# Reordering the last chunks of a recurrence's first stretch, with shared move queues and the weights' low parts on another engine

## The chip, the core and the metric

The kernel runs on one core of a Trainium2 chip. Its engines are TensorE (PE), VectorE (DVE), ScalarE (ACT), GpSimd (POOL) and SyncE (SP); each works through its own queue of instructions in order. SP issues most DMA transfers, ACT a few; an issue takes its place in the queue of the engine that makes it. The metric is the device time of one execution in microseconds (us), as the median of several runs.

## What is computed

```python
# gated recurrence, state 48x48 for each of 4 batches x 8 heads, 768 steps
state = alpha[:, :, t, :, None] * state + einsum('bhd,bhe->bhde', k[:, :, t], v[:, :, t])
y[:, :, t] = einsum('bhd,bhde->bhe', q[:, :, t], state)
x = y as (3072 tokens, 384)
h = x @ w_in                                  # 384 -> 2048
x = (h * sigmoid(h)) @ w_out                  # 2048 -> 384
out = (sigmoid(x @ w_gate) * (x @ w_val)) @ w_out2   # 384 -> 1536 -> 384
```

Everything is float32. The weights arrive as 64-bit numbers and are turned into float32 on the chip.

## The kernel before

**Chunks.** The recurrence is cut into 24 chunks of 128 tokens. For a chunk `c`, `prep` multiplies keys and queries by decay products (two scans and a product on DVE, the queries' product on POOL for the first nine chunks). `full_scores` makes the transposed keys and the scores on PE, `full_scores_done` masks the scores on DVE (line 478) and copies the keys on ACT (line 481), and `full_results` makes the chunk's output `y` and its state update `u` on PE (lines 496 to 517). `full_state` (lines 530 and 533) takes `u` over into the state on DVE and so frees its PSUM place. `y_out` copies `y` to SBUF on ACT (line 552); after each second chunk it also issues six small DMAs, the moves (line 560), which bring 16 rows each to other partitions. `x_out` then splits the two chunks' output into a high part (ACT, line 578, which waits for the moves) and a low part (DVE, line 579).

**First stretch.** Chunks 0 to 8 (`LEAD` is 9) run with whole chunks, 0 to 5 in a loop, and 6, 7 and 8 in code of their own. Queue order is exactly the order of the code (`manual_schedule`). The block of chunk 7 (`c = LEAD - 2`) begins with `x_out(c - 2)`, which is for chunks 4 and 5; that of chunk 8 begins with the first matmul group of the MLP for token block 0 (`early`), and holds `x_out(c - 1)` for chunks 6 and 7.

**Mixed stretch.** Then PE runs the first MLP for token blocks 0 and 1 in an alternating list of 26 items (b, f), f being one of 16 slices of the hidden width: nine matmuls of `mm_in` give `h` (three for each of three slices of the input, high and low parts), ACT makes the Silu `g` (line 741) and its high part `gh` (749), DVE the low part `gl` (750), and nine matmuls of `mm_out` add to the output two items later. Block 1 is made of chunks 4 to 7, so the second group needs what both `x_out` calls give. The pool of `h` has two places, shared with `u` and the transposed keys.

**Weights.** Meanwhile `way1` converts one pair of weight tiles after another: `in` slice j and `out` slice j-1. ACT scales (line 629), DVE rebuilds the number (lines 635 and 637; then, after ACT's line 656, lines 668, 670 and 671), ACT rounds to the high part (line 660, two instructions), POOL subtracts to get the low part (line 678, two instructions). In the first stretch this goes by `bit()`, a quarter of a pair, and in the mixed stretch by `half()`, half a pair at each item, with extra halves after the items in `MORE`. `way2` does the same for the second MLP's weights, much later.

Of the kernel before, what the change touches and what calls it, by code (L numbers as in the profile page):

```python
# [7 lines left out]
F32 = mybir.dt.float32  # L8
# [6 lines left out]
ALU = mybir.AluOpType  # L15
# [23 lines left out]
LEAD = 9  # L39
# [2 lines left out]


BITS = 4
MORE = (3, 10, 16)

FIRST = {"T": (1, 11, 0), "scores": (1, 12, 0)}
VISIT = {9: (1, 12, 1), 10: (1, 13, 0), 11: (1, 14, 0)}
# [139 lines left out]
def gated_attention_then_mlps(ctx: ExitStack, tc: tile.TileContext, qka, a0, v, w_in, w_out, w_gate, w_val, w_out2, out):  # L188
    nc = tc.nc
# [15 lines left out]
    def X(i, dtype=F32):  # L205

        return xp.tile([P, NK, N], dtype, tag=f"x{i}", name=f"x{i}", bufs=1)
# [21 lines left out]
    def load_decays(c):  # L229

        if c < NC:
            qk[c] = places[c % 4]
            nc.sync.dma_start(out=qk[c][:, K_OFF:], in_=qka[c][:, K_OFF:])

    def load_queries(c):
        nc.sync.dma_start(out=qk[c][:, :K_OFF], in_=qka[c][:, :K_OFF])
# [9 lines left out]
    def load_values(c):  # L246
        vt[c] = ap.tile([P, H, D], F32, tag="v", name="v", bufs=4)
        nc.sync.dma_start(out=vt[c], in_=v[c].rearrange("t (h e) -> t h e", e=D))
# [20 lines left out]
    def two_banks(g):  # L269
        return ps_g[g].tile([P, 2, N], F32, tag="s", name=f"s{g}")  # L270
# [14 lines left out]
    def check(c, i):  # L285

        x = (Gt, At)[i].pop(c, None)
        if x is None:
            return
        nc.scalar.activation(x, x, AF.Square, accum_out=chk[:DP, c, i : i + 1])  # L290
# [34 lines left out]
    def last_of(c):  # L325
        return c % CB == CB - 1
# [126 lines left out]
    def full_scores(c, g, p0=0, p1=NP):  # L453

        t = qk[c]
        if p0 == 0:
            S[c] = two_banks(g)
            if not last_of(c):
                T[c] = ps_h.tile([P, N], F32, tag="h", name="t")
        for p in range(p0, p1):  # L460
            if not last_of(c):
                nc.tensor.transpose(T[c][:, p * DP : (p + 1) * DP], t[:, NP * C + p * C : NP * C + (p + 1) * C], ident)
        for p in range(p0, p1):
            for j in range(2):
                r = 64 * j
                nc.tensor.matmul(
                    S[c][:, j, p * C : (p + 1) * C],
                    t[r : r + D, NP * C + p * C : NP * C + (p + 1) * C],
                    t[r : r + D, p * C : (p + 1) * C],
                    start=True,  # L470
                    stop=True,
                )

    def full_scores_done(c):
        for_all = causal.rearrange("s (i t) -> s i t", i=1).to_broadcast([P, NP, C])
        M[c] = M_lead[c % 2]
        for j in range(2):
            nc.vector.tensor_tensor(M[c][j], S[c][:, j].rearrange("s (i t) -> s i t", i=NP), for_all, op=ALU.mult)
        if not last_of(c):
            KT[c] = ap.tile([P, NP, DP], F32, tag="kt", name="kt", bufs=2)  # L480
            nc.scalar.activation(KT[c], T.pop(c)[:, : NP * DP].rearrange("t (p d) -> t p d", p=NP), AF.Copy)
        check(c, 0)
        check(c, 1)

# [50 lines left out]
    def block_of(c):  # L535
        for b, (t0, n) in enumerate(BLOCKS):
            if t0 <= c * C < t0 + n:
                return b, c * C - t0
        raise ValueError(c)
# [3 lines left out]
    def y_out(c):  # L543

        m, o = divmod(c, 2)
        if o == 0:
            xf[m] = ap.tile([P, NP, 2, C], F32, tag="x", name="x", bufs=2)
        x = xf[m]
        if c < LEAD:
            y = Y.pop(c)[:DP].rearrange("r (p t) -> r p t", p=NP)  # L550
            for lo, hi in ((NK, NP), (0, NK)):
                nc.scalar.activation(x[:DP, lo:hi, o], y[:, lo:hi], AF.Copy)
        else:
            y_halves(c, x, o)
        if o:
            for j in range(2):
                r = 64 * j
                for i in range(NK):
                    by = nc.scalar if j and c in (LEAD - 2, LEAD + 2) else nc.sync
                    by.dma_start(out=x[r + D : r + 64, i], in_=x[r + 16 * i : r + 16 * (i + 1), NK])  # L560

    def y_halves(c, x, o):

        yu = YU.pop(c)[0][:, :, :UA].rearrange("r h (p t) -> r h p t", p=NP)
        nc.scalar.activation(x[:DP, :, o, :HC], yu[:DP, 0], AF.Copy)
        for j in range(2):
            r, at = 64 * j, 64 * (1 - j)
            nc.scalar.activation(x[r : r + D, :, o, HC:], yu[at : at + D, 1], AF.Copy)

    def x_out(c):  # L570
        if c % 2 == 0:
            return
        b, o = block_of(c - 1)
        if o == 0:
            xh[b], xl[b] = (X(i, F32R) for i in x_at[b])
        x = xf.pop(c // 2)[:, :NK].rearrange("r k c t -> r k (c t)")
        h, l = (y[b][:, :, o : o + 2 * C] for y in (xh, xl))
        nc.scalar.activation(h, x, AF.Copy, accum_out=chk[:, c, 2:3])
        nc.vector.tensor_tensor(l, x, h.bitcast(F32), op=ALU.subtract)


# [8 lines left out]
    SW = NK * P  # L590

    class Way:
# [80 lines left out]
        def b_rest(self, j):  # L673
            if self.has(j):
                _, _, b, _ = self.views(j)
                for i, key in enumerate(self.pairs[j]):
                    h, l = (wslot[key][:, x].rearrange("p k c -> p (k c)") for x in range(2))
                    nc.gpsimd.tensor_tensor(l, b[:, i * SW : (i + 1) * SW].bitcast(F32), h.bitcast(F32), op=ALU.subtract)  # L678
                self.raw.pop(j), self.tmp.pop(j)

        def bit(self):
# [37 lines left out]
    def mm3(ps, w, k, x_h, x_l, first, last):  # L719

        wh, wl = w[:, 0, k, :], w[:, 1, k, :]
        nc.tensor.matmul(ps, wh, x_l, start=first, stop=False)  # L722
        nc.tensor.matmul(ps, wh, x_h, start=False, stop=False)  # L723
        nc.tensor.matmul(ps, wl, x_h, start=False, stop=last)  # L724
# [7 lines left out]
    def mm_in(pool, tag, name, b, f):  # L732
        h = pool.tile([P, N], F32, tag=tag, name=tag)
        for k in range(NK):
            mm3(h, wslot[name, f], k, xh[b][:, k, :], xl[b][:, k, :], k == 0, k == NK - 1)
        return h
# [86 lines left out]
    with tc.manual_schedule():  # L823
        way1 = Way(
            [[key for key in (("in", j), ("out", j - 1)) if 0 <= key[1] < NF1] for j in range(NF1 + 1)],
            lambda j: X(2 * j % 4, U32).rearrange("p k t -> p (k t)"),
            lambda j: X(2 * j % 4 + 1, U32).rearrange("p k t -> p (k t)"),
            lambda n: wp.tile([P, 2, NK, P], F32R, tag="w", name="w"),
        )
# [41 lines left out]
        def states():  # L871
            while late and (late[0] + 1 == LEAD or last_of(late[0]) or late[0] + 1 in AE):
                c = late.pop(0)
                if not last_of(c):
                    full_state(c)
# [6 lines left out]
        for s in range(4):  # L882
            prep(1, s)
        full_scores_done(0)

        def computed(c):
            full_results(c, c % 2)
            late.append(c)

        def taken(c):  # L890
            load_queries(c + 4)
            load_values(c + 4)
            y_out(c)

        for c in range(LEAD - 3):
            full_scores(c + 1, (c + 1) % 2)
            load_decays(c + 5)
            if c > 2:
                states()
            prep(c + 2, 0)  # L900
            states()
            for s in range(1, 4):
                prep(c + 2, s)
            full_scores_done(c + 1)
            if c > 1:
                x_out(c - 2)
            computed(c)
            if c == 2:
                way1.a_scalar(0)
            taken(c)  # L910
            if c == 0:
                way1.load(1)
            if c > 2:
                way1.bit()


        c = LEAD - 3
# [4 lines left out]
        prep(c + 2, 0)  # L922
        prep(c + 2, 1)
        computed(c)
        states()
        prep(c + 2, 2)
        prep(c + 2, 3)
# [2 lines left out]


        c = LEAD - 2
        x_out(c - 2)
        computed(c)
        way1.bit()
        full_scores(c + 1, (c + 1) % 2)
        load_decays(c + 5)
        taken(c)
        states()
        way1.bit()  # L940
        full_scores_done(c + 1)


        c = LEAD - 1
        early = {(0, 0): mm_in(ps_h, "h", "in", 0, 0)}
        computed(c)
        x_out(c - 1)
        way1.bit()
        states()
        taken(c)  # L950
        for _ in range(3):
            way1.bit()
        way1.n_half = 2 * (way1.n_bits // BITS)

        def steps(items):

# [81 lines left out]
        for i, (b, f) in enumerate(items):  # L1038
# [7 lines left out]
            h = early.pop((b, f), None) or mm_in(ps_h, "h", "in", b, f)  # L1046
# [9 lines left out]
            others(i, 1)  # L1056
            if i in MORE:
                way1.half(True)
# [81 lines left out]
```

## Time and profile before

| what | value |
|---|---|
| median of 3 runs | 960.63 us (959.96 to 961.23) |
| the profiled execution | 961.75 us, of which 959.9 us are the span of its instructions |
| PE busy | 930.9 us (97%) |
| DVE busy | 457.2 us (48%) |
| ACT busy | 391.0 us (41%) |
| POOL busy | 114.7 us (12%) |
| mean granted clock of PE | 0.989 of 2.4 GHz |

Times of rows count from the first instruction. In a timeline row stand start, duration, engine, line, operation, output and inputs, and in brackets how long the engine had been idle before and what released it. SPq and ACTq are DMA issues in those engines' queues.

### The profile page before, as it was taken

What the parts mean: (1) busy time and instruction counts of PE and PEld (TensorE: products, weight loads), DVE (VectorE), ACT (ScalarE), POOL (GpSimd) and SP (SyncE); (2) the same over time, 40 slices, a digit from 0 to 9 for tenths busy, and PEclk for the clock granted to TensorE, in tenths of its full rate; (3) what the DMA queues carried; (4) which work ended last, traced back from release to release, by engine and by line L of the source; (5) the groups of instructions that cost most, each with busy time, mean ns of one, the idle gap of its engine ahead of it and who ended that gap; (6) DMA issues with size and microseconds to landing.
All of it is one profiled execution on the core that took longest, in us unless ns stands there. A gap on an engine that the chain in (4) does not pass through costs nothing.

```text
span 959.9 us, 14882 instructions
## 1 busy us (share of the span) xinstructions
PE 930.9 (97%) x6164; PEld 763.8 (80%) x6164; DVE 457.2 (48%) x682; ACT 391.0 (41%) x725; POOL 114.7 (12%) x109
## 2 busy tenths in 40 slices
PE   7869999999999999999999999999999999999997
PEld 5647888787888888878888888888888888888885
DVE  8858999545534444514675444433222232232221
ACT  3447666454444444435566444433122222222211
POOL 3224444100000000000322111110000000000000
PEclk8989999999999999999999999999999999999999
DMA  9763232041221120004222212001000000000001
GB/s 230 206 181 132 99 104 78 23 119 38 60 62 39 42 59 3 5 1 136 99 93 73 66 66 67 1 1 66 1 0 34 1 1 12 22 1 1 33 1 36
DMA packets 35355, 54.95 MB, mean 57 GB/s; under 512 B 3856, under 2 KB 24368, under 8 KB 35280
## 3 DMA queue, kind: packets, MB, share of 16 engines
q1 hardware_dynamic: 34704, 53.47, 18.6%
q8 instruction: 50, 0.82, 0.4%
q10 hardware_dynamic: 576, 0.46, 0.2%
q14 instruction: 25, 0.20, 0.1%
HBM read 48.02 MB, written 4.72 MB: 55 GB/s over the span
## 4 chain that ended last, share of the span: by engine, by line
PE 88%; DVE 4%; DMA 3%; issue 2%; POOL 1%; ACT 1%; SPq 0%; DVEq 0%; ACTq 0%; POOLq 0%
PE h L722 13%; PE h L724 13%; PE h L723 13%; PE s L722 5%; PE s L724 5%; PE s L723 5%; PE o L724 3%; PE o L722 3%; PE o L723 3%; PE v L722 3%; PE v L723 3%; PE v L724 3%; PE y L722 3%; PE y L724 3%; PE y L723 3%
## 5 line engine op out<-in xcount | busy, mean ns | idle before, releaser
L722 PE MATMUL h<-x,w 128*128 128x512 f32 x582 | 229.5, 394 | 8.5 <-DVE state L533 3.7
L724 PE MATMUL h<-x,w 128*128 128x512 f32 x582 | 228.0, 392 | 1.0 <-POOL w L678 1.0
L723 PE MATMUL h<-x,w 128*128 128x512 f32 x582 | 228.2, 392 | 0.0
L750 DVE TENSOR_TENSOR gl<-g,gh 128x512 fp32r<-128x512 f32 x168 | 123.7, 736 | 191.6 <-ACT gh L749 191.6
L749 ACT ACTIVATE gh<-g 128x512 fp32r<-128x512 f32 x168 | 106.2, 632 | 160.4 <-DVE g L744 157.4
L722 PEld LDWEIGHTS h<-x,w 128*128 128x128 f32 x582 | 110.0, 189 | 33.2 <-DVE state L533 3.9
L724 PEld LDWEIGHTS h<-x,w 128*128 128x128 f32 x582 | 110.1, 189 | 25.0 <-POOL w L678 1.5
L723 PEld LDWEIGHTS h<-x,w 128*128 128x128 f32 x582 | 110.2, 189 | 22.9
L744 DVE TENSOR_TENSOR g<-v,g 128x512 f32<-128x512 f32 x46 | 31.8, 692 | 178.7 <-PE v L724 178.7
L741 ACT ACTIVATE g<-h 128x512 f32<-128x512 f32 x96 | 56.9, 593 | 128.9 <-PE h L724 128.9
L743 ACT ACTIVATE g<-h 128x512 f32<-128x512 f32 x72 | 43.1, 598 | 136.3 <-PE h L724 136.3
L722 PE MATMUL s<-gl,w 128*128 128x512 f32 x240 | 95.4, 398 | 0.1
L724 PE MATMUL s<-gh,w 128*128 128x512 f32 x240 | 93.6, 390 | 0.0
L723 PE MATMUL s<-gh,w 128*128 128x512 f32 x240 | 93.6, 390 | 0.0
L678 POOL TENSOR_TENSOR w<-tmp,w 128x384 fp32r<-128x384 f32 x36 | 40.9, 1158 | 207.4 <-ACT w L660 207.4
L678 POOL TENSOR_TENSOR w<-x,w 128x384 fp32r<-128x384 f32 x32 | 50.0, 1579 | 70.5 <-ACT w L660 70.5
L722 PE MATMUL o<-gl,w 128*128 128x512 f32 x144 | 56.2, 390 | 0.0
L724 PE MATMUL o<-gh,w 128*128 128x512 f32 x144 | 56.2, 390 | 0.0
L723 PE MATMUL o<-gh,w 128*128 128x512 f32 x144 | 56.1, 390 | 0.0
L744 DVE TENSOR_TENSOR g<-h,g 128x512 f32<-128x512 f32 x26 | 18.0, 691 | 79.8 <-PE h L724 79.8
L722 PE MATMUL v<-x,w 128*128 128x512 f32 x138 | 54.0, 391 | 0.0
L723 PE MATMUL v<-x,w 128*128 128x512 f32 x138 | 53.9, 390 | 0.0
(141 smaller groups left out, 1288.6 us busy)
## 6 DMA issues: line engine op xcount, KB each, us to landing
x<-in_moe_w_in SPq DMA_DIRECT2D x16, 384.0 KB, 3.4
x<-in_moe_w_out SPq DMA_DIRECT2D x16, 384.0 KB, 3.8
x<-in_qka SPq DMA_DIRECT2D x12, 448.0 KB, 4.4
qk<-in_qka SPq DMA_DIRECT2D x11, 448.0 KB, 6.1
v<-in_v SPq DMA_DIRECT2D x24, 192.0 KB, 4.9
raw<-in_moe_w_gate SPq DMA_DIRECT2D x12, 384.0 KB, 3.8
raw<-in_moe_w_val SPq DMA_DIRECT2D x12, 384.0 KB, 3.8
raw<-in_moe_w_out SPq DMA_DIRECT2D x12, 384.0 KB, 3.8
```

The lines of the kernel that those rows point to most:

```text
L678: nc.gpsimd.tensor_tensor(l, b[:, i * SW : (i + 1) * SW].bitcast(F32), h.bitcast(F32), op=ALU.subtract)
L722: nc.tensor.matmul(ps, wh, x_l, start=first, stop=False)
L723: nc.tensor.matmul(ps, wh, x_h, start=False, stop=False)
L724: nc.tensor.matmul(ps, wl, x_h, start=False, stop=last)
L741: nc.scalar.activation(g, h, AF.Silu)
L743: nc.scalar.activation(g, h, AF.Sigmoid)
L744: nc.vector.tensor_tensor(g, val, g, op=ALU.mult)
L749: nc.scalar.activation(gh, g, AF.Copy)
L750: nc.vector.tensor_tensor(gl, g, gh.bitcast(F32), op=ALU.subtract)
```

## The change

It has three parts. Its own line numbers stand 2 to 8 above those of before: 533 becomes 535, 552 554, 560 562, 578 580, 579 587, 629 637, 635 643, 637 645, 656 664, 660 668, 668 676, 670 678, 671 679, 678 686, 741 749, 749 757, 750 758.

1. Order in the last chunks. For chunk 7, `x_out(5)` moves behind `computed(7)` and a conversion quarter, and its DVE half is put off to chunk 8 (`x_rest`); `y_out(7)` goes ahead of the loads of chunks 11 and 12. For chunk 8, a conversion quarter and `states()` go ahead of `x_out(7)`; two quarters are left out and become half a pair in the mixed stretch (`n_half` 3 in place of 4, `MORE` with four entries). The squares that check overflow (`checks`) go behind `y_out(8)` for chunk 8.
2. Of the six moves after chunks 1, 3 and 5, three are now issued by ACT, as was so after chunk 7.
3. The weights' low parts are subtracted by DVE for all pairs but the first of each way.

```diff
-MORE = (3, 10, 16)
+MORE = (3, 10, 15, 21)
...
-                    by = nc.scalar if j and c in (LEAD - 2, LEAD + 2) else nc.sync
+                    by = nc.scalar if j and (c < LEAD or c == LEAD + 2) else nc.sync
...
-    def x_out(c):
+    def x_out(c, rest=None):
...
+        if rest is not None:
+            rest.append((l, x, h))
+        else:
+            x_rest(l, x, h)
+
+    def x_rest(l, x, h):
         nc.vector.tensor_tensor(l, x, h.bitcast(F32), op=ALU.subtract)
...
-                    nc.gpsimd.tensor_tensor(l, b[:, i * SW : (i + 1) * SW].bitcast(F32), h.bitcast(F32), op=ALU.subtract)
+                    (nc.vector if j else nc.gpsimd).tensor_tensor(l, b[:, i * SW : (i + 1) * SW].bitcast(F32), h.bitcast(F32), op=ALU.subtract)
...
         c = LEAD - 2
-        x_out(c - 2)
         computed(c)
         way1.bit()
+        rest = []
+        x_out(c - 2, rest)
         full_scores(c + 1, (c + 1) % 2)
+        y_out(c)
         load_decays(c + 5)
-        taken(c)
+        load_queries(c + 4)
+        load_values(c + 4)
         states()
         way1.bit()
         full_scores_done(c + 1)
...
         c = LEAD - 1
+        x_rest(*rest[0])
         early = {(0, 0): mm_in(ps_h, "h", "in", 0, 0)}
+        way1.bit()
         computed(c)
+        states()
         x_out(c - 1)
         way1.bit()
-        states()
         taken(c)
-        for _ in range(3):
-            way1.bit()
-        way1.n_half = 2 * (way1.n_bits // BITS)
+        way1.a_scalar(2)
+        checks(c)
+        way1.n_half = 3
```

PE's own order does not change. DVE's order from chunk 8's second scan on, before (`state` by 533 frees chunk 7's `u`, 530 chunk 8's; the two 579 are `x_out` for chunks 5 and 7):

```order
L316 SCALAR_TENSOR_TENSOR A<-qk_92,d_89 112x512
L579 TENSOR_TENSOR x_635<-x,x_634 128x3x256
L635 TENSOR_SCALAR x_666<-x_666 128x768
L533 TENSOR_TENSOR state_88<-u,aend 112x192
L637 SCALAR_TENSOR_TENSOR x_666<-x_666 128x768
L478 TENSOR_TENSOR m_98<-s_669,causal 128x512
L478 TENSOR_TENSOR m_99<-s_669,causal 128x512
L579 TENSOR_TENSOR x_635<-x,x_634 128x3x256
L668 TENSOR_SCALAR x_666<-x_666 128x768
L670 TENSOR_TENSOR x_666<-x_666 128x768
L671 TENSOR_TENSOR x_666<-x_666 128x768
L530 COPY state_88<-u 112x192
```

and the same place of the change:

```order
L316 SCALAR_TENSOR_TENSOR A<-qk_92,d_89 112x512
L643 TENSOR_SCALAR x_662<-x_662 128x768
L535 TENSOR_TENSOR state_88<-u,aend 112x192
L645 SCALAR_TENSOR_TENSOR x_662<-x_662 128x768
L478 TENSOR_TENSOR m_98<-s_668,causal 128x512
L478 TENSOR_TENSOR m_99<-s_668,causal 128x512
L587 TENSOR_TENSOR x_666<-x,x_665 128x3x256
L676 TENSOR_SCALAR x_662<-x_662 128x768
L678 TENSOR_TENSOR x_662<-x_662 128x768
L679 TENSOR_TENSOR x_662<-x_662 128x768
L532 COPY state_88<-u 112x192
L587 TENSOR_TENSOR x_666<-x,x_665 128x3x256
```

The subtraction for chunk 5 moved behind the state of chunk 7 and the masks of chunk 8, and that for chunk 7 behind the conversion and the state of chunk 8.

ACT's order from `x_out` for chunk 5 to the first Silu, before:

```order
L578 ACTIVATE x_634,chk<-x 128x3x256
L629 ACTIVATE x_666<-x_242 128x768
L552 ACTIVATE x<-y_638 112x128
L552 ACTIVATE x<-y_638 112x3x128
L560 DMA x<-x 16x256 x3
L656 ACTIVATE x_666<-x_242 128x768
...
L578 ACTIVATE x_634,chk<-x 128x3x256
L660 ACTIVATE w<-x_666 128x384 x2
...
L656 ACTIVATE x_763<-x_511 128x768
L741 ACTIVATE g<-h 128x512
```

and in the change:

```order
L637 ACTIVATE x_662<-x_242 128x768
L580 ACTIVATE x_665,chk<-x 128x3x256
L554 ACTIVATE x<-y_634 112x128
L554 ACTIVATE x<-y_634 112x3x128
L562 DMA x<-x 16x256 x3
L664 ACTIVATE x_662<-x_242 128x768
L481 ACTIVATE kt<-t 128x448
L668 ACTIVATE w<-x_662 128x384 x2
L580 ACTIVATE x_665,chk<-x 128x3x256
...
L290 ACTIVATE A,chk<-A 112x512
L749 ACTIVATE g<-h 128x512
```

The scaling by 629 now stands ahead of the wait for chunk 5's moves, the rounding to high parts ahead of the wait for chunk 7's, and no line 656 stands right ahead of the first Silu; two checks stand there.

On DVE, one round of the mixed stretch before (one pair, two items):

```order
L668 TENSOR_SCALAR x_780<-x_780 128x768
L670 TENSOR_TENSOR x_780<-x_780 128x768
L671 TENSOR_TENSOR x_780<-x_780 128x768
L750 TENSOR_TENSOR gl<-g,gh 128x512
L635 TENSOR_SCALAR x_829<-x_829 128x768
L637 SCALAR_TENSOR_TENSOR x_829<-x_829 128x768
L750 TENSOR_TENSOR gl<-g,gh 128x512
```

and in the change:

```order
L676 TENSOR_SCALAR x_761<-x_761 128x768
L678 TENSOR_TENSOR x_761<-x_761 128x768
L679 TENSOR_TENSOR x_761<-x_761 128x768
L758 TENSOR_TENSOR gl<-g,gh 128x512
L686 TENSOR_TENSOR w<-x_761,w 128x384 x2
L643 TENSOR_SCALAR x_796<-x_796 128x768
L645 SCALAR_TENSOR_TENSOR x_796<-x_796 128x768
L758 TENSOR_TENSOR gl<-g,gh 128x512
```

The two subtractions stand in DVE's queue behind each second `gl`; POOL's queue has none of them.

## Rows read from the trace of the kernel before

**Rows 1.** Timeline of PE, four idle times around the first `h` groups:

```profile
53.43 1.16 PE L466 MATMUL s<-qk 48*128 48x128 f32 x16
58.34 0.79 PE L722 MATMUL h<-x,w 128*128 128x512 f32 x1 [3.75 <-DVE state L533]
...
64.17 1.08 PE L517 MATMUL y<-qk,state 48*64 48x128 f32 x16
68.38 0.80 PE L722 MATMUL h<-x,w 128*128 128x512 f32 x1 [3.12 <-DVE state L530]
...
73.60 0.50 PE L722 MATMUL h<-x,w 128*128 128x512 f32 x1 [1.30 <-ACT g L741]
```

**Rows 2.** Busy time by stretch: PE, PEld, DVE, ACT, POOL, then PEclk, DMA share, GB/s:

```profile
34.10:51.80 17.70, 14.06 (x194) 11.35 (x192) 17.53 (x28) 8.91 (x26) 3.44 (x4) 0.90 0.88 235
68.40:71.80 3.40, 3.40 (x8) 2.73 (x9) 1.36 (x2) 1.97 (x5) 1.97 (x2) 0.50 0.06 19
73.60:168.00 94.40, 94.33 (x414) 77.56 (x414) 88.79 (x109) 64.70 (x113) 44.17 (x29) 1.00 0.32 105
400.00:760.00 360.00, 359.74 (x1741) 295.99 (x1740) 155.15 (x225) 144.78 (x239) 40.89 (x36) 1.00 0.14 47
```

**Rows 3.** Timeline of ACT between chunk 7 and the first Silu:

```profile
55.62 0.84 ACT L578 ACTIVATE x<-x 128x768 fp32r<-128x768 f32 x1 [5.58 <-DMA x<-x]
56.47 0.89 ACT L629 ACTIVATE x<-x 128x768 f32<-128x768 f32 x1
57.26 0.64 ACT L552 ACTIVATE x<-y 112x128 f32<-112x128 f32 x2
57.55 1.90 ACTq L560 DMA_DIRECT2D x<-x  x3
59.49 0.91 ACT L656 ACTIVATE x<-x 128x768 bf16<-128x768 uint16 x1 [1.59 <-DVE x L637]
...
60.73 0.62 ACT L290 ACTIVATE G<-G 112x512 f32<-112x512 f32 x1
...
64.07 0.84 ACT L578 ACTIVATE x<-x 128x768 fp32r<-128x768 f32 x1 [2.02 <-DMA x<-x]
68.09 0.94 ACT L660 ACTIVATE w<-x 128x384 fp32r<-128x384 f32 x2 [3.08 <-DVE x L671]
72.96 0.58 ACT L741 ACTIVATE g<-h 128x512 f32<-128x512 f32 x1
```

**Rows 4.** Timeline of DVE in the same stretch:

```profile
57.94 0.35 DVE L533 TENSOR_TENSOR state<-u,aend 112x192 f32<-112x192 f32 x1
65.04 0.96 DVE L579 TENSOR_TENSOR x<-x,x 128x768 fp32r<-128x768 f32 x1 [4.69 <-ACT x L578]
```

**Rows 5.** Timeline of SP, the six moves after chunk 5:

```profile
46.04 6.92 SPq L560 DMA_DIRECT2D x<-x  x6
```

**Rows 6.** Groups of DVE from 73.6 to 170: count, busy us, mean ns, idle before:

```profile
L750 DVE TENSOR_TENSOR gl<-g,gh 128x512 fp32r<-128x512 f32 x24 | 23.1, 962 | 1.4 <-ACT gh L749 1.4
L637 DVE SCALAR_TENSOR_TENSOR x<-x 128x768 uint32<-128x768 uint32 x13 | 19.4, 1493 | 0.4
L671 DVE TENSOR_TENSOR x<-x 128x768 f32<-128x768 f32 x14 | 13.4, 958 | 0.5
...
L670 DVE TENSOR_TENSOR x<-x 128x768 bf16<-128x768 bf16 x14 | 7.8, 558 | 1.8 <-ACT x L656 0.4
```

**Rows 7.** Timelines of POOL and of DVE, with and without POOL at work:

```profile
75.52 2.76 POOL L678 TENSOR_TENSOR w<-x,w 128x384 fp32r<-128x384 f32 x2 [4.86 <-ACT w L660]
75.75 1.65 DVE L637 SCALAR_TENSOR_TENSOR x<-x 128x768 uint32<-128x768 uint32 x1
97.69 0.96 DVE L637 SCALAR_TENSOR_TENSOR x<-x 128x768 uint32<-128x768 uint32 x1
98.57 0.69 DVE L750 TENSOR_TENSOR gl<-g,gh 128x512 fp32r<-128x512 f32 x1
```

**Rows 8.** From PE's waits over the span (total, times, longest):

```profile
PE h L724 <- POOL w L678: 1.0, 1, 1.0
```

More of the change, by code (lines that the diff above doesn't have):

```diff
@@ L481, in full_scores_done, with checks @@
             nc.scalar.activation(KT[c], T.pop(c)[:, : NP * DP].rearrange("t (p d) -> t p d", p=NP), AF.Copy)
+    def checks(c):
         check(c, 0)
@@ L884, in gated_attention_then_mlps @@
         full_scores_done(0)
+        checks(0)
         def computed(c):
@@ L904, in gated_attention_then_mlps @@
             full_scores_done(c + 1)
+            checks(c + 1)
             if c > 1:
@@ L924, in gated_attention_then_mlps @@
         computed(c)
+        checks(c + 1)
         states()
```

## Prediction

> **What bounds the kernel now.** I read PE's waits first, then PE's timeline at the places they name, then ACT's and DVE's timelines there. From 73.6 to 168 us PE is busy 94.33 of 94.40 us at full clock [rows 2], and over the whole span the list of its waits names little behind that but one wait of 1.0 us for a low part of the weights, late in the mixed stretch [rows 8]. So time can be won only ahead of 73.6, and at that one wait. Ahead of 73.6 PE stands idle three times: 3.75 us ahead of the first `h` group, 3.12 ahead of the second, 1.30 ahead of the third [rows 1]. The first two groups also run slowly: the second takes 73.60 - 1.30 - 68.38 = 3.92 us, the granted clock from 68.4 to 71.8 being 0.50, 1.2 GHz [rows 2]; at full clock nine matmuls take 9 x 94.40 / 414 = 2.05 us.
>
> Why PE waits is seen on ACT and DVE. The scores of chunk 8 are done at 54.59 [rows 1], but `u` of chunk 7 is freed only at 57.94 + 0.35 [rows 4]: DVE's subtraction for chunk 5 stands ahead of it and waits for ACT's line 578, which waits 5.58 us for chunk 5's moves [rows 3]. The same wait holds `y_out(7)` on ACT, at 57.26, and so chunk 7's moves, the second 578 (64.07), the second 579 (65.04), and behind it the conversion and the state, which end PE's second wait. The third is for the Silu at 72.96, which stands behind two line-656 jobs and their DVE work. In the stretch before, 34.1 to 51.8, DVE is busy 17.53 of 17.70 us [rows 2]: the loop's last chunks are bound by DVE, and the change leaves DVE's order there alone. I therefore give nothing to part 2 of the change before 51.8.
>
> **The change, step by step.** (a) *When `y_out(7)` starts.* Chunk 7's `y` is ready before the scores of chunk 8 are, so 57.26 is set by the landing at 55.62, then 578 (0.85 to the next start) and 629 (0.79) [rows 3]. The 629 now runs during the wait. The landing itself: SP needs 6.92 us for six issues [rows 5], over 1.1 each, because it waits for earlier transfers, and ACT took 1.90 for three [rows 3]. With half the moves on ACT, SP could be free some 3.4 us sooner; but the stretch from 34.1 to 51.8 has the DMA engines at 0.88 [rows 2], so the moves stand behind loads already on their way. The landing moves by between 0 and 2.7 us (then ACT is free for `y` when it comes); I take 0.3, near the lower end for that row. `y_out(7)` starts at 55.3 + 0.85 = 56.2.
>
> The Trainium skill, "DMA: Bandwidth & Descriptors", section "Issuing engines are not separate DMA queues", says that DMAs from any engine end on the same 16 DMA engines and interleave, so spreading them saves issue time alone. By that rule the landing stays at 55.62, the gain of this step is 0.8 us in place of 1.1, and the whole comes to 953.9, so it is no case apart.
>
> (b) *From `y_out(7)` to the second `h` group.* Before: 68.38 - 57.26 = 11.12 us. Now, on ACT: from line 552 to the start of 656 as in the trace, 59.49 - 57.26 = 2.23, the three issues in it; 656 0.91. DVE's 670 and 671: 0.56 + 0.96 [rows 6]. ACT's 660 pair 0.94, then 578 for chunk 7, 65.04 - 64.07 = 0.97, then DVE's 579 0.96 [rows 3, 4]. Sum 7.5 us, so the second group can begin at 56.2 + 7.5 = 63.7. Chunk 7's moves must have landed by 61.8, 5.6 us behind `y_out(7)`; the trace shows 64.07 - 57.26 = 6.8, with the loads of chunk 12 and some of chunk 11 issued ahead of SP's three. These now stand behind, so I take the 61.8; with 6.8 it is 1.2 later. The new order of `states()` costs nothing: its copy waits for `u` of chunk 8 and lies between 671 and 579, while ACT works. What was cover for SP, the loads put behind the moves, isn't needed before the mixed stretch is well under way. The first `h` group follows the scores at 54.6 with no idle time; this alone would gain nothing, since the second is later anyway.
>
> (c) *From the second group to the third.* The third waits for PE, and for the Silu: from the end of 578 (62.75) line 552 0.54, 629 0.79, two checks at 0.62 each, 741 0.58 [rows 3], done at 65.9. The second group ends at 63.7 + 2.05 = 65.8 at full clock or 63.7 + 3.92 = 67.6 at 1.2 GHz. PE has then been idle for about 2.3 us (`y` of chunk 8 can't end before about 61.4, behind 656 and the keys' copy at 59.8). In the trace 3.12 us of idle time were followed by 1.2 GHz, 1.30 were not [rows 1, 2]. I take the slow one: third group at 67.6 in place of 73.60, 6.0 us won by (a) to (c); at full clock 7.7.
>
> (d) *The mixed stretch.* DVE gets 29 subtractions of 128x384 there. The nearest rows are 0.69 for 128x512 [rows 7] and 0.96 for 128x768 [rows 4]; on the line through both, 0.54; 0.69 is the upper bound, half of 0.96 the lower. That is 15.7 us of work. It loses the stretches of waiting for POOL: line 637 takes 1.65 beside POOL and 0.96 alone [rows 7], its mean being 1.49, and `gl` 0.96 in place of 0.69 [rows 6]. 13 x 0.53 + 24 x 0.27 = 13.4 us. Net 2.3 us more, and DVE has 94.40 - 88.79 = 5.6 us to spare [rows 2]. Ahead of the subtractions DVE must wait for ACT's pair of 660 (0.94), but `gl` (0.69) lies in that time; where ACT is still at 629 it waits longer, so 0.1 a pair, 14 pairs, 1.4 us. The half pair that moved here from the first stretch is DVE's 635 and 637, 1.5 us. So DVE just holds, with 5.6 - 2.3 - 1.4 - 1.5 = 0.4 us to spare, and PE waits for nothing new. Bounds: with 0.48 each there are 1.7 us more, with 0.69 PE waits some 4 us. On the other side the low parts are ready sooner: 1.1 us behind the high parts where POOL takes 2.76 for the pair [rows 7]. The wait of 1.0 us goes [rows 8].
>
> The Trainium skill, "SBUF — State Buffer", section "Who interferes with whom", says that only DVE and GpSimd share a port, as an exclusive lock. By that rule the long forms of 637 and `gl` go altogether, as (d) has it; were they DVE's own, the sum would be the fourth case below. The rows of 637 agree with the rule.
>
> (e) *The rest.* The second MLP's 34 subtractions on DVE (18 us by the same price) lie between 400 and 760, where DVE is busy 155 of 360 us and PE 359.74 [rows 2]: hidden, and two items lie between a `gl` and its use.
>
> Sum: 6.0 + 1.0 = 7.0 us. The profiled execution took 961.75 (span 959.9 and 1.85 around it), so 954.75; the median of the runs shown is 1.12 lower, so **953.6**.
>
> **Rivals.** *Early moves.* ACT's issues are not held, the moves land up to 2.7 us sooner, and PE keeps the full clock: 2.4 and 1.7 us more, 949.5. For it: SP's slow issues [rows 5]. Against: DMA at 0.88. *ACT held.* The issues on ACT wait for earlier transfers as SP's do, 1.15 us each in place of 0.63: 1.6 us more behind chunk 7 on the path, and with the 6.8 us of (b) 1.2 more, 956.4. For it: nothing says that SP's wait is SP's own. Against: ACT's three took 1.90 in the trace. *DVE paces the mixed stretch, partly.* At 0.69 a piece or with ACT late for each pair, PE waits 2 to 5 us there: 955.6 to 958.6. *The other side.* The long forms of 637 and `gl` are not POOL's doing: then 15.7 + 1.4 + 1.5 us of work meet 5.6 of room, PE waits 13 us, and the kernel takes 960.63 - 6.0 + 13.0 = 967.6. It is slower than before as soon as a pair costs DVE some 0.5 us (7.0 / 14) more than the 1.2 taken here. Against it: 0.96 and 1.65 for the same instruction [rows 7].
>
> **How the numbers follow.** Forecast 0.54 (its own range 951.5 to 955.5), early moves 0.13, ACT held 0.15, DVE partly 0.11, the other side 0.07. The range reaches from the first rival, 949.5, past ACT held to the middle of the fourth, 957.5. Below about 958.7 is faster by over 0.2%, about what a measurement can tell from no change: all of the first three, and most of DVE partly, 0.88; within it 0.05; slower 0.07.
>
> **What would show it.** The `h` group for item (0, 0) begins right behind the scores at about 54.6 (right for the 533 that moved); the second at about 63.7, the third between 66 and 68; `y_out(7)` near 56.2, its start right behind 578. If the moves' landing for chunk 5 is much before 55, (a) is wrong. In the mixed stretch 637 and `gl` have one duration each, 0.96 and 0.69, the subtraction 0.5 to 0.6, and PE has no wait for `g`, `gl` or weights. PE waits there in pieces of over a microsecond would make the prediction wrong, and so would a second group held by chunk 7's moves.

## The result, and the profile after

The changed kernel takes 950.0 us (median of five, 948.63 to 952.29), the kernel before 959.96 beside it: a ratio of 0.99, with an interval of 0.9877 to 0.9923. The forecast was 953.6 with a range of 949.5 to 957.5. A later sitting with the same kernel gave 951.22 (950.15 to 953.52; 0.9924, interval 0.9908 to 0.994), so 8.9 to 10.0 us were won, where 7.0 had been worked out.

The profiled execution takes 948.63 us, 13.1 less than that of before; it is 1.4 us below the median of its runs, and that of before 1.8 above its own. The page's first lines split this: PE is busy 3.1 us less (930.9 before), and idle 19.0 us of the span where it was idle 29.0.

```profile
span 946.8 us, 14844 instructions
...
PE 927.8 (98%) x6164; PEld 762.0 (80%) x6164; DVE 466.8 (49%) x747; ACT 390.8 (41%) x725; POOL 28.3 (3%) x44
```

PE's timeline at the places of [rows 1]:

```profile
51.82 1.16 PE L466 MATMUL s<-qk 48*128 48x128 f32 x16
52.91 0.50 PE L730 MATMUL h<-x,w 128*128 128x512 f32 x1
...
57.91 1.08 PE L519 MATMUL y<-qk,state 48*64 48x128 f32 x16
60.88 0.47 PE L730 MATMUL h<-x,w 128*128 128x512 f32 x1 [1.89 <-DVE x L587]
...
62.78 0.40 PE L732 MATMUL h<-x,w 128*128 128x512 f32 x1
63.02 0.39 PE L730 MATMUL h<-x,w 128*128 128x512 f32 x1
```

In this execution the first `h` group follows the scores with no idle time (3.75 before), the second comes at 60.88 in place of 68.38 behind 1.89 us of idle time (3.12), the third at 63.02 in place of 73.60 with none (1.30). ACT's timeline, to set beside [rows 3]:

```profile
52.46 0.85 ACT L580 ACTIVATE x<-x 128x768 fp32r<-128x768 f32 x1 [3.25 <-DMA x<-x]
...
53.30 0.64 ACT L554 ACTIVATE x<-y 112x128 f32<-112x128 f32 x2
53.59 1.82 ACTq L562 DMA_DIRECT2D x<-x  x3
55.46 0.91 ACT L664 ACTIVATE x<-x 128x768 bf16<-128x768 uint16 x1 [1.51 <-DVE x L587]
...
57.98 0.94 ACT L668 ACTIVATE w<-x 128x384 fp32r<-128x384 f32 x2 [1.18 <-DVE x L679]
58.83 0.83 ACT L580 ACTIVATE x<-x 128x768 fp32r<-128x768 f32 x1
...
62.20 0.58 ACT L749 ACTIVATE g<-h 128x512 f32<-128x512 f32 x1
```

Chunk 5's moves free line 580 at 52.46, 3.2 us sooner than in [rows 3], and `y_out(7)` follows at 53.30. From there to the second group it is 60.88 - 53.30 = 7.58 us, where 11.12 stood before. The second 580 waits for no move; it stands right behind the two rounding instructions of line 668. The 1.51 us ahead of 664 are ACT's own three issues: they last until 55.41. On DVE the state's update for chunk 7 stands at 51.45, ahead of chunk 5's subtraction (line 587, at 54.23) and no longer behind it. First the row of before that stands ahead of the 533 of [rows 4], then the changed kernel's:

```profile
56.59 0.96 DVE L579 TENSOR_TENSOR x<-x,x 128x768 fp32r<-128x768 f32 x1 [4.78 <-ACT x L578]
```

```profile
51.45 0.36 DVE L535 TENSOR_TENSOR state<-u,aend 112x192 f32<-112x192 f32 x1 [0.81 <-issue]
...
54.23 0.95 DVE L587 TENSOR_TENSOR x<-x,x 128x768 fp32r<-128x768 f32 x1
...
59.78 0.96 DVE L587 TENSOR_TENSOR x<-x,x 128x768 fp32r<-128x768 f32 x1 [0.37 <-ACT x L580]
60.65 1.02 DVE L686 TENSOR_TENSOR w<-x,w 128x384 fp32r<-128x384 f32 x2
```

Windows as in [rows 2], one around the second group first:

```profile
60.90:64.30 3.40, 3.40 (x15) 2.83 (x16) 3.02 (x6) 3.37 (x9) 0.00 (x0) 1.00 1.05 319
...
73.60:168.00 94.40, 94.40 (x421) 78.16 (x420) 84.99 (x135) 63.02 (x112) 1.33 (x3) 1.00 0.28 90
400.00:760.00 360.00, 359.74 (x1740) 295.76 (x1739) 165.26 (x258) 142.75 (x235) 2.71 (x2) 1.00 0.14 47
```

The second group runs at full clock (fifteen matmuls in 3.40 us, where [rows 2] have eight at 0.50). Between 400 and 760 us DVE is busy 165.26 us (155.15 before) and PE 359.74 as before, so the second MLP's subtractions are hidden, as step (e) has it. And DVE's groups from 73.6 to 170, as in [rows 6]:

```profile
L758 DVE TENSOR_TENSOR gl<-g,gh 128x512 fp32r<-128x512 f32 x24 | 16.4, 685 | 4.9 <-ACT gh L757 4.9
L686 DVE TENSOR_TENSOR w<-x,w 128x384 fp32r<-128x384 f32 x26 | 13.4, 555 | 1.4 <-ACT w L668 1.4
L645 DVE SCALAR_TENSOR_TENSOR x<-x 128x768 uint32<-128x768 uint32 x12 | 11.5, 958 | 0.4
```

With POOL nearly out of the stretch (1.33 us busy, 44.17 before), `gl` takes 0.685 us (0.962) and line 645 0.958 (1.493); the subtraction takes 0.555.

### The profile page after: what moved, and what is told of

Same layout as the page of the kernel before. It is cut to its first block, busy times and chain, and to the rows that moved or that the text cites. A ratio compares the mean times of both kernels' runs of the same rounds, so it can differ in the third digit from the quotient of the medians.

```text
span 946.8 us, 14844 instructions
## 1 busy us (share of the span) xinstructions
PE 927.8 (98%) x6164; PEld 762.0 (80%) x6164; DVE 466.8 (49%) x747; ACT 390.8 (41%) x725; POOL 28.3 (3%) x44
## 4 chain that ended last, share of the span: by engine, by line
PE 94%; DMA 3%; DVE 1%; issue 1%; ACT 1%; SPq 0%; ACTq 0%; POOL 0%; DVEq 0%
PE h L730 14%; PE h L731 14%; PE h L732 14%; PE s L730 6%; PE s L731 6%; PE s L732 6%; PE o L732 3%; PE o L730 3%; PE o L731 3%; PE v L730 3%; PE v L731 3%; PE v L732 3%; PE y L730 3%; PE y L732 3%; PE y L731 3%; DMA x<-x 1%
## 5 line engine op out<-in xcount | busy, mean ns | idle before, releaser
L758 DVE TENSOR_TENSOR gl<-g,gh 128x512 fp32r<-128x512 f32 x168 | 115.9, 690 | 186.8 <-ACT gh L757 186.8
L730 PE MATMUL v<-x,w 128*128 128x512 f32 x138 | 53.9, 391 | 0.0
L731 PE MATMUL v<-x,w 128*128 128x512 f32 x138 | 53.8, 390 | 0.0
L732 PE MATMUL v<-x,w 128*128 128x512 f32 x138 | 53.7, 389 | 0.0
L730 PEld LDWEIGHTS s<-gl,w 128*128 128x128 f32 x240 | 45.0, 188 | 9.9
L732 PEld LDWEIGHTS s<-gh,w 128*128 128x128 f32 x240 | 45.0, 188 | 9.6
```

The source lines that it names most:

```text
L758: nc.vector.tensor_tensor(gl, g, gh.bitcast(F32), op=ALU.subtract)
```

## The experiments

Times are medians against runs of the kernel before on the same chip (960.1, in all three sittings), with the interval of the ratio.

**Part 2 undone.** Lines of the changed kernel:

```diff
-                    by = nc.scalar if j and (c < LEAD or c == LEAD + 2) else nc.sync
+                    by = nc.scalar if j and c in (LEAD - 2, LEAD + 2) else nc.sync
```

> The changed kernel with part 2 undone: all six moves of chunks 1, 3 and 5 are issued by SP again. The changed kernel takes 950.0, the kernel before 960.0. Theory of the prediction (part 2 moves the landing of chunk 5's moves by about 0.3 us, the rest of the 3.2 us by which it came sooner is the new order and the state of the DMA engines): 950.3 to 951, the second `h` group within 0.5 us of 60.9. Rival (the split queue itself brings the landing 3 us forward, and takes away DVE's 2.24 us of waiting for chunk 1's moves at line 587): 952.5 to 954, ACT's line 580 for chunk 5 near 55.3, the second `h` group near 63.5.

951.48 us (948.93 to 955.15; 0.9893 to 0.9927): between the two theories, with a spread that covers both. The profiled execution was its slowest, 955.15. In it the moves came at 54.70 and the second group at 63.97; moreover PE had a granted clock of 0.50 (half clock) for some ten microseconds (window), which began with `u` and `y` of chunk 8, ahead of the second group:

```profile
59.80:69.90 10.10, 8.64 (x46) 6.97 (x44) 7.15 (x12) 8.04 (x17) 0.00 (x0) 0.50 0.81 239
```

**Part 3 undone.**

```diff
-                    (nc.vector if j else nc.gpsimd).tensor_tensor(l, ...)
+                    nc.gpsimd.tensor_tensor(l, ...)
```

> The changed kernel with part 3 undone: the low parts of the weights of the second and later ways are subtracted by POOL again. Theory of the prediction (d): in the mixed stretch line 645 takes 1.65 us beside POOL again and `gl` 0.96, PE's wait of about 1 us for a low part returns, and the second half-pair that moved into the stretch meets a DVE with 5.6 us to spare: 1 to 1.5 us slower than the changed kernel, 951 to 951.5. Rival (part 3 does nothing for the time, the wait having gone with the earlier start of the stretch): within 0.3 us of 950.0.

953.63 us (0.9921 to 0.9949): 2.4 to 3.6 slower than the changed kernel's two medians, more than either theory had. PE's waits, then the windows of this kernel:

```profile
PE h L732 <- POOL w L686: 2.3, 2, 1.2
```

```profile
73.60:140.00 66.40, 66.40 (x294) 54.88 (x294) 64.43 (x78) 45.09 (x78) 32.86 (x22) 1.00 0.35 115
140.00:164.00 24.00, 21.71 (x94) 16.90 (x93) 22.75 (x28) 15.52 (x29) 11.66 (x8) 1.00 0.15 50
```

and DVE's groups from 73.6 to 170:

```profile
L758 DVE TENSOR_TENSOR gl<-g,gh 128x512 fp32r<-128x512 f32 x24 | 23.0, 960 | 2.6 <-ACT gh L757 2.6
L645 DVE SCALAR_TENSOR_TENSOR x<-x 128x768 uint32<-128x768 uint32 x12 | 19.1, 1596 | 0.4
```

Both long forms are back, DVE is busy 64.43 of 66.40 us, and later PE waits twice for a low part, 2.3 us together. Ahead of that stretch, chunk 7's subtraction runs beside POOL's and takes 1.57 us in place of 0.96, so the second group begins 8.16 us behind `y_out(7)` (62.65 - 54.49), 0.6 more than in the changed kernel:

```profile
60.93 1.57 DVE L587 TENSOR_TENSOR x<-x,x 128x768 fp32r<-128x768 f32 x1 [0.37 <-ACT x L580]
```

**Part 3 alone**, the same line in the kernel before.

> The kernel before with part 3 alone: low parts of the second and later ways subtracted by DVE behind the high parts. Theory of the prediction (d): PE's wait of 1.0 us goes, nothing else: 1.0 us faster than before, 958.7 to 959.2. Rival (DVE has no room: a pair costs it more than 1.2 us): slower than before, by 2 us and more. Second rival (longer forms also held DVE in the first stretch, so part 3 gives more): 957 or less.

959.53 us (0.998 to 1.0002), 0.6 faster by the medians and within what can be told from nothing. The one wait of 1.0 us [rows 8] is not in this trace. By the medians part 3 is worth little by itself and 2.4 us or more with the new order.

The traces don't show that difference. From the third `h` group to the end of the span it is 886.3 us before (959.9 - 73.60) and 884.0 with part 3 alone (955.1 - 71.11); with the new order 886.8 and 887.7 where POOL subtracts (part 1 alone, part 3 undone) and 883.8 and 884.3 where DVE does (the changed kernel, twice). So behind the third group part 3 takes off 2.3 us in the old order and 2.5 to 3.9 in the new one (part 1 alone still has some half clock there). Why the median with part 3 alone shows only 0.6 of it stays open; its profiled execution, 957.1, was 2.4 us faster than its median.

**Part 2 alone**, its line in the kernel before.

> The kernel before with part 2 alone: one of each two halves of the moves of chunks 1, 3 and 5 is issued by ACT. Theory of the prediction (a): landing of chunk 5's moves 0.3 us sooner, nothing before 51.8 us: 959.5 to 960. Rival (the split queue gives the early landing by itself): line 578 for chunk 5 near 52.5 in place of 55.62, DVE's wait at the first line 579 gone, 956.5 to 958. Second rival (ACT is held by waits for earlier transfers): slower than before by 1 us and more.

960.75 us (0.9994 to 1.0016): no gain. ACT's timeline tells why even an earlier landing would not pay here:

```profile
54.54 0.84 ACT L578 ACTIVATE x<-x 128x768 fp32r<-128x768 f32 x1 [4.66 <-DMA x<-x]
...
64.15 0.84 ACT L578 ACTIVATE x<-x 128x768 fp32r<-128x768 f32 x1 [3.27 <-DMA x<-x]
```

Chunk 5's moves come at 54.54, 1.1 sooner than in [rows 3], but chunk 7's at 64.15, as late as before (64.07): they stand behind the loads that the old order puts ahead of them, and line 578 waits 3.27 us for them in place of 2.02.

**Part 1 alone**, the changed kernel with both edits above.

> Part 1 of the change alone: the new order of the last chunks, with the moves all on SP and the low parts on POOL. So far: the changed kernel 950.0, without part 2 951.5, without part 3 953.6, part 2 alone 960.75, part 3 alone 959.5, before 960.1. Theory A (part 2 is worth nothing that can be told from run to run; part 3 is worth 3.6 us with the new order and 0.6 without it, since the half pair that moved into the mixed stretch makes DVE and POOL too late there): 953.5 to 955. Theory B (the effects simply add): 950.0 + 1.5 + 3.6 = 955.1 by the one side, 960.1 - (10.1 - 0.6 + 0.6) = 950.0 by the other, so the four numbers can't add and the value lies at one of these ends, 950 or 955; at 951 or less part 3 would be needless.

955.51 us (0.9929 to 0.9966), half a microsecond above the upper end of both theories: 4.6 us for the order alone. Putting part 3 to it gives 4.0 more (951.48), part 2 alone 1.9 (953.63). Its timelines of ACT, of PE and of DVE:

```profile
56.01 0.64 ACT L554 ACTIVATE x<-y 112x128 f32<-112x128 f32 x2
```

```profile
59.59 0.90 PE L510 MATMUL u<-state,ident 48*64 48x192 f32 x4 [2.39 <-ACT kt L481]
...
61.44 1.97 PE L519 MATMUL y<-qk,state 48*64 48x128 f32 x16
64.86 0.76 PE L730 MATMUL h<-x,w 128*128 128x512 f32 x1 [1.46 <-DVE x L587]
```

```profile
63.46 0.36 DVE L532 COPY state<-u 112x192 f32<-112x192 f32 x1 [2.77 <-PE y L519]
63.76 0.96 DVE L587 TENSOR_TENSOR x<-x,x 128x768 fp32r<-128x768 f32 x1
```

`y_out(7)` at 56.01 is near the 56.2 of the forecast, but the second group, at 64.86, comes 1.2 us later than its 63.7 and 8.85 us behind `y_out(7)`. Another path ends last here: PE waits 2.39 us for ACT's copy of the keys, then does `u` and `y` of chunk 8 at a granted clock of 0.50 (line 519 takes 1.97 us, 1.08 in the changed kernel), and the state's copy (line 532), which the new order puts ahead of the second subtraction, comes only at 63.46. Part 2 undone has the same in its first execution (8.43 us, a wait of 1.89, line 519 at 1.97).

**DVE's room.** In the changed kernel, DVE does the second subtraction of each pair of the first MLP's weights twice:

```diff
+                    if j and i and self is way1:
+                        nc.vector.tensor_tensor(l, b[:, i * SW : (i + 1) * SW].bitcast(F32), h.bitcast(F32), op=ALU.subtract)
```

> The changed kernel, in which DVE does the second of each pair's subtractions of the first way twice: some 14 x 0.555 = 7.8 us more DVE work in the mixed stretch, nothing else. Theory of the prediction (d) (DVE just holds, 0.4 us to spare): PE waits some 7 us there, 957. Rival from the trace of the changed kernel (DVE's gaps between 68 and 164 us add up to 6.3 us and are all usable): PE waits 1.5 us, 951.5. Second rival (there is more room, since the wait of DVE for ACT's line 757 is short only by chance): within 0.5 us of 950.0.

957.54 us (0.9958 to 0.9983), near the 957 of the forecast's theory. The trace has 15 doubled subtractions, not 14: 15 x 0.558 = 8.4 us more of DVE work cost 6.3 to 7.5 us against the changed kernel's two medians. PE's waits and two windows:

```profile
PE h L732 <- ACT w L668: 3.6, 3, 1.7
```

```profile
140.00:164.00 24.00, 21.14 (x91) 16.30 (x89) 22.75 (x37) 15.35 (x29) 0.00 (x0) 1.00 0.17 61
164.00:170.00 6.00, 6.00 (x20) 4.63 (x19) 5.79 (x12) 3.63 (x8) 0.00 (x0) 0.72 0.00 1
```

DVE is busy 22.75 of 24 us here, as with part 3 undone, where PE waits too. Behind the longest wait, 1.67 us, PE's granted clock falls: 20 matmuls in 6.00 us, where at the full clock's 94.40 / 421 = 0.224 us each they take 4.5. That is 1.5 us of the loss which are not DVE's time. So by estimate 0.9 (8.4 - 7.5) to 3.6 us (8.4 - 6.3 + 1.5) were to spare, where the forecast had 0.4, and the 6.3 us of gaps that the expectation counts on DVE are not all free room.

**`y_out(7)` behind the loads again**, in the changed kernel (the loads are those of chunk 11, not 10 as the expectation says).

```diff
-        y_out(c)
         load_decays(c + 5)
         load_queries(c + 4)
         load_values(c + 4)
+        y_out(c)
```

> The changed kernel with `y_out(7)` behind the loads again, as in the kernel before: the moves of chunk 7 that SP issues stand behind the loads of chunk 10's queries and values. Theory of the prediction (b) (the loads ahead of the moves cost what the trace of before showed, moves landed 6.8 us behind `y_out(7)` in place of 3.9 in the changed one): line 580 for chunk 7 waits some 1.5 us, the second `h` group comes 1.5 us later, idle time ahead of it 3.4 us; 951.5, and 953.2 if the granted clock falls to 0.50 for that group. Rival (line 580 stands behind the conversion of the weights anyway): within 0.5 us of 950.0.

954.37 us (0.9922 to 0.9959): 3.2 to 4.4 lost, the larger theory and more. ACT and PE:

```profile
62.11 0.84 ACT L580 ACTIVATE x<-x 128x768 fp32r<-128x768 f32 x1 [2.39 <-DMA x<-x]
```

```profile
64.18 0.74 PE L730 MATMUL h<-x,w 128*128 128x512 f32 x1 [4.39 <-DVE x L587]
```

Line 580 for chunk 7 waits 2.39 us for the moves, the second group comes 3.3 us later behind 4.39 us of idle time, and its clock is 0.50 (0.74 us for a first matmul in place of 0.47).

**That one order in the kernel before.** The opposite test: `taken(7)` there with `y_out` first.

```diff
+        y_out(c)
         load_decays(c + 5)
-        taken(c)
+        load_queries(c + 4)
+        load_values(c + 4)
```

> The kernel before, in which only `y_out(7)` moves ahead of the loads of chunk 10's queries and values (lines 940 to 942 of the listing). Theory of the prediction (b) (without the loads ahead, chunk 7's moves land 5.6 us behind `y_out(7)` in place of 6.8): 1.2 us sooner, 958.8. Theory from the changed kernel with `y_out(7)` behind the loads (4.4 us lost, of which 3.3 were the landing): 956 to 957.5. Rival (DVE's line 579 for chunk 5 and the conversions hold the second group anyway): 960.

958.18 us (0.9971 to 0.9997), 1.9 won, between the two theories (the loads are chunk 11's here too). ACT and PE:

```profile
59.38 0.83 ACT L578 ACTIVATE x<-x 128x768 fp32r<-128x768 f32 x1
```

```profile
63.67 0.50 PE L722 MATMUL h<-x,w 128*128 128x512 f32 x1 [2.46 <-DVE state L530]
68.90 0.50 PE L722 MATMUL h<-x,w 128*128 128x512 f32 x1 [1.64 <-ACT g L741]
```

Line 578 no longer waits for chunk 7's moves, but the conversion and the state's update (line 530) behind it on DVE now end PE's wait, and the wait for the Silu stays.

**The other half of the order alone.** In the kernel before, only chunk 5's subtraction moves behind the scores of chunk 8.

```diff
-        x_out(c - 2)
+        rest = []
+        x_out(c - 2, rest)
...
         c = LEAD - 1
+        x_rest(*rest[0])
```

> The kernel before, in which only DVE's subtraction for chunk 5 (line 579) moves behind the scores of chunk 8, so that the state's update that frees `u` of chunk 7 no longer stands behind the wait for the moves. Theory of the prediction (b) (the first `h` group comes some 3.7 us sooner, right behind the scores, and the second doesn't): 960, the idle time ahead of the second group some 3 us longer. Rival (what PE does ahead of the second group also comes sooner and the chain behind with it): 957 to 958.5.

960.23 us (0.9989 to 1.0011), as the forecast's step (b) says: no gain. PE:

```profile
58.47 0.80 PE L728 MATMUL h<-x,w 128*128 128x512 f32 x1 [2.07 <-DVE state L533]
...
68.82 0.50 PE L728 MATMUL h<-x,w 128*128 128x512 f32 x1 [2.14 <-DVE state L530]
```

The first group still waits 2.07 us, since a step of the conversion that waits for ACT, behind the same moves, now stands ahead of line 533. So it did not come right behind the scores, nor did the idle time ahead of the second group grow, as the expectation had both: the time came out as expected, but the reason given for it was not put to the test.

**`y_out(7)` ahead of `x_out(5)` too**, an attempt at a faster kernel.

```diff
         rest = []
+        y_out(c)
         x_out(c - 2, rest)
         full_scores(c + 1, (c + 1) % 2)
-        y_out(c)
...
-        x_rest(*rest[0])
         early = {(0, 0): mm_in(ps_h, "h", "in", 0, 0)}
         way1.bit()
+        x_rest(*rest[0])
```

> The changed kernel with `y_out(7)` also ahead of `x_out(5)`, so that on ACT it no longer stands behind the wait for chunk 5's moves, and with chunk 5's subtraction (line 587) behind the conversion of the weights on DVE. Theory (the chain from `y_out(7)` and from the conversion of the weights sets the second `h` group): ACT does `y_out(7)` at 51.4 and its three issues during its wait of 3.25 us, line 664 starts at 54.9 in place of 55.5, the second `h` group some 0.6 to 1.0 us sooner; 949.0 to 949.5. Rival (ACT's issues hold line 580 for chunk 5, and all behind it comes later): 950.5 to 951.5. Second rival (the gain is lost to PE's own work ahead of the group): 950.0.

950.56 us (0.9883 to 0.9919): no gain. ACT's row shows the first rival, 1.64 us of waiting for its own issues ahead of line 580. The second group begins at 60.69, no later than in the changed kernel (60.88 and 61.92), but the window around it shows the half clock, and the third comes at 64.36 (63.02 and 64.08):

```profile
54.22 0.85 ACT L580 ACTIVATE x<-x 128x768 fp32r<-128x768 f32 x1 [1.64 <-issue]
```

```profile
60.60:63.90 3.30, 3.21 (x8) 2.57 (x9) 2.92 (x6) 3.27 (x8) 0.00 (x0) 0.50 0.89 293
```

**The changed kernel again, with part 2 and without it.**

> The changed kernel once more, unchanged, for a second profile and more times. 949.5 to 951. Theory (the profile of before and that of after differ by some 3 us more than the medians, since one execution's transfers in the first 30 us ran 1.5 to 2 us sooner than the other's): the landing of chunk 5's moves lies between 52.4 and 53.6 here, and the second `h` group moves with it, 60.9 to 62.1. Rival (the landing near 52.4 belongs to the kernel): within 0.2 us of the first profile.

> The changed kernel without part 2 once more, beside the changed kernel on the same chip. So far 951.5 against 950.0, with runs from 948.9 to 955.2. Theory A (part 2 is worth about 1.7 us once the new order is there, as the pair without part 3 also shows, 955.5 against 953.6): 951.5 to 952. Theory B (0.3 us, as the prediction had it): 950 to 950.7.

951.22 us with, 951.6 (948.28 to 952.25; 0.9891 to 0.9928) without. The time without lies in the range of theory A, the difference of 0.4 is nearer to theory B. ACT's line 580 and PE's second group of the changed kernel in this execution:

```profile
53.50 0.85 ACT L580 ACTIVATE x<-x 128x768 fp32r<-128x768 f32 x1 [3.19 <-DMA x<-x]
```

```profile
61.92 0.47 PE L730 MATMUL h<-x,w 128*128 128x512 f32 x1 [1.89 <-DVE x L587]
```

The whole stretch is 1.0 us later than in the first profile, with the same 1.89 us of idle time. So the landing near 52.4 does not belong to the kernel. Without part 2, line 580 stands at 53.43 in this sitting, no later than with it.

## Why the prediction was right, and where it was off

**Step (a), when `y_out(7)` starts: the right wait, but its landing mis-sized.** The landing was to move by 0.3 us, and by the prediction's own sign (a) is wrong if it comes much before 55: the changed kernel's two profiles have 52.46 and 53.50. One profile on either side says 3.2 us, but executions differ, and the 55.62 of before was one of the late ones. With half of the moves on ACT, the line that waits for chunk 5's moves starts at 52.46, 53.50, 53.64, 52.69, 53.27 and 54.54 (mean 53.35; the changed kernel twice, then part 3 undone, DVE's room, `y_out` behind the loads, part 2 alone; the attempt is left out, since its own issues hold the line). With all on SP it is 55.62, 54.70, 53.43, 53.51, 55.16, 55.85 and 53.07 (mean 54.48; before, part 2 undone twice, part 3 alone, part 1 alone, and the two halves of the order). So about 1.1 us of the 3.2 fit part 2. Two executions of one kernel differ by 1.0 and 1.3 us, kernels that issue these moves alike by up to 2.8; the rest of the 3.2 is the luck of the two executions, and part of why the profiles differ by 13.1 us and the medians by 9 to 10. What part 2 is worth in time isn't settled: 1.9 us between the medians without part 3, 1.5 and 0.4 with it, none alone. ACT's issues were not held: three take 1.82 us after chunk 7. SP's half of the issues after chunk 5 now takes, by SP's timeline, 4.13 us for three:

```profile
46.34 4.13 SPq L562 DMA_DIRECT2D x<-x  x3
```

so SP is done with them at 50.47, where [rows 5] end at 52.96. Over the same profiles as above SP is done at 51.8 on average with the split and at 52.4 without it: its three issues still take 1.2 to 1.4 us each, and begin later (47.9 against 45.1 on average). By SP's waits at that line, the three issues of the changed kernel wait 3.3 us for three earlier transfers, as the six of before did (3.4): the waits stayed with SP. So of the 3.4 us by which (a) had SP free sooner, 0.6 came. The Trainium skill, "DMA: Bandwidth & Descriptors", section "Issuing engines are not separate DMA queues", was read in the prediction as leaving the landing where it was. That was too narrow, since the section grants the time saved on issuing. The means lean to an earlier landing, but the spread within a kind is larger than their difference.

**Step (b), `y_out(7)` to the second group: right for the changed kernel.** 7.5 us were forecast; the changed kernel has 7.58 in both profiles, by the chain that was added up (`y_out`, issues, 664, 668, 580, 587). That the new order of `states()` costs nothing holds there, but not in general: with part 1 alone, and in one execution with part 2 undone, the state's copy came late and it was 8.85 and 8.43 us. The part of the order that makes it is `y_out(7)` ahead of the loads: moved back alone it costs 3.2 to 4.4 us, where the prediction priced it at 1.2. There the price was wrong at one end: line 580 stands 62.11 - 54.12 = 7.99 us behind `y_out(7)` with the loads ahead, where 6.8 was taken, and 58.83 - 53.30 = 5.53 without them, close to the 5.6 taken; the conversion sets it there and not the moves. That is 2.5 us, and the half clock behind the longer wait took 1.6 more. That the split of `x_out(5)` gains nothing alone was borne out by the time, not by a test of its reason.

**Step (c), the third group: the clock was taken wrongly for the changed kernel.** PE stood idle for 1.89 us (2.3 forecast) and the second group ran at full clock in both its profiles, which is the 1.7 us that (c) left open. Without part 2 the same 1.89 us were followed by half clock in one execution (window):

```profile
61.80:65.10 3.30, 3.21 (x8) 2.59 (x9) 2.91 (x5) 3.27 (x8) 0.00 (x0) 0.50 1.05 329
```

so the length of the idle time, by which (c) chose the slow case (3.12 us slow, 1.30 not), doesn't decide it; what does, these runs don't show. The third group needs no wait for the Silu, which is done by 62.78.

**Step (d), the mixed stretch: right, and it carries more than its term says.** The subtraction takes 0.555 us (0.54 forecast), both long forms are gone, PE has no wait for weights, and DVE has little room, by the doubled subtractions. The long forms are POOL's doing: they come back with its work alone. The Trainium skill, "SBUF — State Buffer", section "Who interferes with whom", states the exclusive lock between DVE and GpSimd; these traces agree that DVE is held up beside POOL (0.960 and 0.685 us for `gl`), while no row tells that the lock is exclusive. The 1.0 us that (d) gave part 3 counts one wait of PE. By the medians part 3 is worth 0.6 us against the old order and 2.4 to 4.0 with the new one, so the new order brings its full gain only with it; the traces, with 2.3 and 2.5 to 3.9 us behind the third group, have it larger than 1.0 in both orders.

**The sum.** 7.0, and 0.8 more for the landing, and 1.7 for the clock, make 9.5 from 960.1: 950.6, between the two medians. This is an estimate after the fact, and that it meets them is in part luck: part 3 stands in it with the 1.0 of (d), the size of part 2 is open, and only two executions of the changed kernel show that they kept the full clock. Both medians lie below the forecast's own range (951.5 to 955.5) and nearer to the first rival, early moves with the full clock (949.5, given 0.13), than to 953.6. Of that rival the full clock came in both profiles; of its 2.7 us for the landing the means show 1.1.

## What to carry to other kernels

Before pricing an earlier start, look at what the next engine can do with it: by the medians the order won 4.6 us by itself and 4 more once DVE was freed from POOL's company, though that freeing alone won 0.6. On an issue queue, a transfer that PE will wait for belongs ahead of loads that nobody needs yet; that was worth more than spreading its issues over two queues. And read one profile against several: the landing of the same transfers differed by 1.0 and 1.3 us between two executions of one kernel.

## What was not expected of the hardware

The idle time of PE directly ahead of the second group did not tell whether that group would run at a granted clock of 0.50: 1.58, 1.89 and 4.39 us were followed by it in three of these traces (the attempt, part 2 undone for the second time, `y_out` behind the loads), 1.89 (the changed kernel twice, and DVE's room), 2.14 (the other half of the order) and 2.50 (part 3 undone) not. In the 61 runs of the kernel before in the three sittings, the mean clock of an execution goes from 0.983 to 0.994. The one at 0.983 took 961.84 us, the three at 0.994 took 957.8 to 958.14: the spread from run to run goes in part with the clock, and what sets it stays open.
